# Three one-bank accumulators in place of one three-bank tile, and one block maximum a bank

## The chip, the cores and the metric

The kernel runs on one core of a Trainium2 chip. The core has a matrix engine (TensorE, PE in the profile, with its weight loads shown apart as PEld), a vector engine (VectorE, DVE), a scalar engine (ScalarE, ACT), GpSimd (POOL) and an engine that only issues DMAs here (SyncE, SP). The metric is the device time of one execution in microseconds; the kernel before takes 995.15 us (median of three runs, 993.82 to 997.5). Matrix products land in PSUM, which the kernel divides into eight banks of 512 float32 values a partition.

## What is computed

Block-sparse attention over 4 batches, 8 heads, 768 positions and head size 64, and then a feed-forward layer over all 3072 tokens:

```
scores = q @ k.T / 8, -1e9 where a 32x32 block isn't allowed
attn   = exp(scores - rowmax); attn /= attn.sum + 1e-9
x      = (attn @ v) as 3072 x 512
h      = x @ w_in                      # 512 x 2048
g      = h * clip(h + 3, 0, 6) / 6
out    = g @ w_out                     # 2048 x 512
```

All in float32. The kernel splits most float32 operands into a high part and a low remainder and adds three products. The subtraction of a row maximum is what the change touches on the attention side: before the exponentials of a head, the kernel needs for each query the largest allowed score, and gets it from maxima over the 24 blocks of 32 keys.

## The kernel before

**Units.** A unit is one head of one batch for one half (384) of its queries: 64 units, `u0` to `u63`. Its operations have short names. `m_0`, `m_1`, `m_2` are two matmuls each (128 queries by 2 times 384 keys); `r_0`, `r_1`, `r_2` are the VectorE reductions that take the 24 block maxima out of each (the tile `bm`); `fin_0` adds the mask row (`mq`), `fin_1` takes the maximum of the maxima (`mneg`); `mt` and `qm` carry it into an extra row of the query operand; `s`, `e` and `av` are scores, exponentials and the product with v; `suma` to `sumc` (tile `acc`) add up the denominator. `ql` (VectorE, tile `QA`) and `kl` (GpSimd, tile `kb`) compute low parts of the operands.

**Steps.** A step `m0` to `m63` is two column blocks of the feed-forward layer for one half of one batch: `h_..` (matmuls into `big`), `ga`, `gb`, `gh`, `gl` (the activation, on ScalarE, VectorE, ScalarE, GpSimd; tiles `g`, `ghi`, `glo`), and `o_tj` for three row tiles t and two blocks j: three matmuls that add into row tile t of the output. Eight steps accumulate into the same three row tiles; after the last of the eight, `oc_t` copies row tile t out of PSUM on VectorE (in the profile the copy `wraw<-out`, since it reuses that buffer), and `od_t` sends it to memory. The eight last steps of a group are `m7`, `m15`, and so on to `m63`.

**Weights.** 32 pieces of weight are taken apart early in the run (`w0` to `w31`, tiles `wraw` and `xhl`); this is VectorE and ScalarE work until about 212 us.

**Order.** The order is written out by hand in the long string SCORE. Each engine runs its instructions strictly in that order, each waiting on semaphores. The semaphores are set by the tile layer: it makes an instruction wait for earlier accesses to the same tile that it must not overtake.

**PSUM.** `big_tile()` gives one of two buffers of two banks (four banks), `avp` one bank, and `outp` three banks. In the kernel before, these three are one tile, `OUT` (`out` in the profile), made once at the top. It has three uses: the accumulators `OUT[:, t]` of the steps; the mask product of `mq` in its third bank; and for the early units `u1` to `u8` (where `self.early` holds) the two score halves of `m_t` in banks 0 and 1, so that these need no `big` buffer. In SCORE every early `m` comes after the `r` before it, since both use the same two banks.

All instructions are recorded through one helper, so nearly every row of the profile has its line (L357); rows are told apart by tile names and shapes.

Of the kernel before, what the change touches and what calls it, by code (L numbers as in the profile page):

```python
# [13 lines left out]
F32 = mybir.dt.float32  # L14
F32R = mybir.dt.float32r
I32 = mybir.dt.int32
AF = mybir.ActivationFunctionType
ALU = mybir.AluOpType
AX = mybir.AxisListType

P = 128
B, H, S, D = 4, 8, 768, 64
BLK = 32
NB = S // BLK
HALF = S // 2
NC = S // P
DM = H * D
# [4 lines left out]
NT = HALF // P  # L32
# [8 lines left out]
SCORE = """  # L41
# [286 lines left out]
def fused_kernel(ctx: ExitStack, tc, qT, kT, vP, sampled, w_in, w_out, krows, table, ident_d, out):  # L328
    nc = tc.nc
    const = ctx.enter_context(tc.tile_pool(name="const", bufs=1))  # L330
    sb = ctx.enter_context(tc.tile_pool(name="sb", bufs=2))
# [3 lines left out]
    outp = ctx.enter_context(tc.tile_pool(name="outp", bufs=1, space=bass.MemoryType.PSUM))  # L335

    def big_tile():
        return big.tile([P, 2, 512], F32, name="big")
# [20 lines left out]
    pe, dve, act, pool, dma = (Ordered(e) for e in (nc.tensor, nc.vector, nc.scalar, nc.gpsimd, nc.sync))  # L359
# [7 lines left out]
    eps_b = const.tile([P, 1], F32, name="eps_b")  # L367
    ones = const.tile([P, 32], F32, name="ones")
    MN = [const.tile([P, 2, NT], F32R, name=f"mneg{i}") for i in range(2)]
    OUT = outp.tile([P, NT, DM], F32, name="out")  # L370
    VO = [const.tile([P, 2 * NC * D], F32, name=f"vo{side}") for side in range(2)]

    def set_constants():
# [36 lines left out]
    class Masks(Work):  # L410
# [8 lines left out]
        def needs(self, op):  # L419
            return [(self, self.NEEDS.get(op, ""))]  # L420

        def heat(self):

            self.hot = sb.tile([P, 2, HALF], F32R, name="ghi")
            nc.gpsimd.memset(self.hot.bitcast(F32), 1.0)

        def warm(self, *number):
            for _ in range(number[-1]):
                pe.matmul(OUT[:, 2, :HALF], lhsT=self.hot[:, 0, :P], rhs=self.hot[:, 1], start=True, stop=True)

        def samp(self):
            self.sampled = const.tile([NB, 6], I32, name="samp")
            dma.dma_start(out=self.sampled, in_=sampled)
# [37 lines left out]
                dve.tensor_scalar(out=self.mval[:, 64:88], in0=msk, scalar1=1.0, scalar2=-NEG, op0=ALU.subtract, op1=ALU.mult)  # L471

        def mq(self):
            self.mqp = OUT[:, 2]
            for t in range(NC):
                pe.matmul(self.mqp[:, t * NB:(t + 1) * NB], lhsT=self.ind_f[:NB, t // NT * HALF + t % NT:(t // NT + 1) * HALF:NT], rhs=self.mval[:, 64:88].bitcast(F32), start=True, stop=True)

# [59 lines left out]
    class Unit(Work):  # L537
# [89 lines left out]

        def m(self, t):
            if self.early:
                ps = OUT[:, 0:2]  # L630
            else:
                ps = big_tile()
            self.mps = [*(self.mps if t else []), ps[:, :, :HALF]]
            for j in range(2):
                pe.matmul(ps[:, j, :HALF], lhsT=self.QA[:, t:HALF:NT], rhs=self.KA[:, j * HALF:(j + 1) * HALF], start=True, stop=True)

        def r(self, t):
            if t == 0:
                self.bm = sb.tile([P, NT, NB], F32, name="bm")
            bm = self.bm[:, t].rearrange("p (j n) -> p j n", j=2)  # L640
            dve.tensor_reduce(out=bm, in_=self.mps[t].rearrange("p j (n e) -> p j n e", e=BLK), axis=AX.X, op=ALU.max)

        def fin(self, i):
            if i == 0:
# [125 lines left out]
    moe_out = {}  # L770

    class Step(Work):
# [74 lines left out]

        def o(self, t, j):
            if self.fp == 0 and t == 0 and j == 0:
                moe_out[self.b, self.hf] = [OUT[:, t_] for t_ in range(NT)]  # L850
            o = moe_out[self.b, self.hf][t]
            f = 2 * self.fp + j
            for i, (lhs, rhs) in enumerate(((self.ghi, wout_hi[:, f]), (self.ghi, self.wo[j]), (self.glo, wout_hi[:, f]))):
                pe.matmul(o, lhsT=lhs[:, j, t * P:(t + 1) * P], rhs=rhs, start=f + i == 0, stop=f + i == NF + 1)
# [13 lines left out]
    masks = Masks()  # L868
# [22 lines left out]
            for op in ops:  # L891
                work.do(op)

    if "warm" in SCORE:
        masks.do("heat")
    set_constants()
    play(SCORE)

# [37 lines left out]
```

## Time and profile before

| | |
|---|---|
| median of three runs | 995.15 us |
| profiled execution, its own time | 994.87 us |
| its span, first to last instruction | 993.1 us |
| TensorE busy | 950.6 us (96%), clock 0.997 |
| VectorE busy | 642.3 us (65%), 900 instructions |
| ScalarE, GpSimd busy | 471.1 us, 249.9 us |
| chain that ended last | PE 80%, DVE 12%, ACT 3% |
| reductions from the early banks, `bm<-out` | 24, 954 ns each, 21.7 to 91.0 us |
| copies out of the accumulators, `wraw<-out` | 24, 686 ns each, 231.1 to 989.5 us |

A timeline row gives start, length, engine, operation, tiles and count, and in brackets the idle time of that engine just before it and whose end ended it. A row of the view of waits gives who waited for whom, the sum in us, how many times, and the longest. A busy TensorE is no proof of full use: matmuls overlap, so their pitch (from one start to the next) says more than their length.

### The profile page before, as it was taken

What the parts mean: (1) busy time and instruction counts of PE and PEld (TensorE: products, weight loads), DVE (VectorE), ACT (ScalarE), POOL (GpSimd) and SP (SyncE); (2) the same over time, 40 slices, a digit from 0 to 9 for tenths busy, and PEclk for the clock granted to TensorE, in tenths of its full rate; (3) what the DMA queues carried; (4) which work ended last, traced back from release to release, by engine and by line L of the source; (5) the groups of instructions that cost most, each with busy time, mean ns of one, the idle gap of its engine ahead of it and who ended that gap; (6) DMA issues with size and microseconds to landing.
All of it is one profiled execution on the core that took longest, in us unless ns stands there. A gap on an engine that the chain in (4) does not pass through costs nothing.

```text
span 993.1 us, 13262 instructions
## 1 busy us (share of the span) xinstructions
PE 950.6 (96%) x4756; PEld 767.9 (77%) x4756; DVE 642.3 (65%) x900; ACT 471.1 (47%) x712; POOL 249.9 (25%) x148
## 2 busy tenths in 40 slices
PE   6898999999999999999999999999999999999997
PEld 4566777778687878878878878887888787778886
DVE  5788898976768654777666674665666675752111
ACT  5787766463445344444553454444354543432121
POOL 3221222322223123232332233122222212302221
PEclk9899999999999999999999999999999999999999
DMA  6676977664444454535454455454543544515442
GB/s 199 193 244 210 273 267 236 202 220 147 144 139 139 123 165 132 155 111 165 142 153 132 131 152 163 124 154 134 170 147 108 149 131 138 145 48 146 142 118 72
DMA packets 103701, 155.48 MB, mean 157 GB/s; under 512 B 32819, under 2 KB 51891, under 8 KB 103636
## 3 DMA queue, kind: packets, MB, share of 16 engines
q1 hardware_dynamic: 103636, 154.64, 51.2%
q8 instruction: 37, 0.61, 0.3%
q14 instruction: 28, 0.23, 0.1%
HBM read 139.63 MB, written 14.78 MB: 155 GB/s over the span
## 4 chain that ended last, share of the span: by engine, by line
PE 80%; DVE 12%; ACT 3%; issue 3%; DMA 1%; POOL 0%; DVEq 0%; ACTq 0%
PE big L357 44%; PE out L357 25%; PE av L357 12%; DVE xhl L357 3%; DVE bm L357 3%; DVE acc L357 2%; DVE QA L357 2%; ACT pr L357 1%; ACT xhl L357 1%; DMA win_lo<-xhl 1%; DMA wout_lo<-xhl 1%; DVE wraw L357 0%; ACT qb L357 0%; DVE uu L357 0%; DMA qraw<-qT 0%
## 5 line engine op out<-in xcount | busy, mean ns | idle before, releaser
L357 PE MATMUL big<-xhl,win_hi 128*128 128x384 f32 x1024 | 265.0, 340 | 0.6 <-DVE bm L357 0.6
L357 POOL TENSOR_TENSOR glo<-g,ghi 128x768 fp32r<-128x768 f32 x64 | 120.2, 1878 | 430.3 <-ACT ghi L357 425.1
L357 ACT ACTIVATE pr<-big 128x768 f32<-128x768 f32 x192 | 153.0, 809 | 102.9 <-PE big L357 102.1
L357 POOL TENSOR_TENSOR kb<-kraw,KA 64x768 fp32r<-64x768 f32 x64 | 124.4, 1943 | 298.8 <-ACT KA L357 252.8
L357 PEld LDWEIGHTS big<-xhl,win_hi 128*128 128x128 f32 x1024 | 184.5, 188 | 14.3 <-issue 7.3
L357 DVE TENSOR_REDUCE bm<-big 128x24 f32<-128x768 f32 x168 | 158.0, 953 | 54.8 <-PE big L357 53.0
L357 PE MATMUL big<-xhl,wlo_in 128*128 128x384 f32 x512 | 172.3, 337 | 0.0
L357 PE MATMUL av<-pr,vo 128*64 128x384 f32 (+1 forms) x768 | 163.6, 494 | 0.1
L357 PE MATMUL out<-wout_hi,ghi 128*128 128x512 f32 x384 | 152.7, 398 | 5.8 <-DVE wraw L357 5.8
L357 PE MATMUL out<-wout_hi,glo 128*128 128x512 f32 x384 | 151.2, 394 | 0.6 <-POOL glo L357 0.6
L357 PE MATMUL out<-wlo_out,ghi 128*128 128x512 f32 x384 | 150.8, 393 | 0.0
L357 PE MATMUL big<-QA,KA 128*128 128x384 f32 x384 | 138.5, 361 | 3.1 <-ACT pr L357 1.3
L357 PE MATMUL big<-qb,kb 97*128 97x384 f32 x384 | 132.7, 345 | 3.9 <-ACT qb L357 3.2
L357 DVE SCALAR_TENSOR_TENSOR g<-g,big 128x768 f32<-128x768 f32 x64 | 60.8, 950 | 109.7 <-ACT g L357 109.3
L357 ACT ACTIVATE g<-big,half_b 128x768 f32<-128x768 f32 x64 | 57.7, 902 | 142.5 <-PE big L357 126.9
L357 PEld LDWEIGHTS av<-pr,vo 128*64 128x64 f32 (+1 forms) x768 | 67.6, 147 | 65.6 <-issue 50.5
L357 PE MATMUL big<-KA,QA 128*128 128x384 f32 x336 | 92.7, 367 | 13.9 <-ACT KA L357 5.1
L357 PEld LDWEIGHTS big<-KA,QA 128*128 128x128 f32 x336 | 74.8, 255 | 35.9 <-issue 8.8
L357 DVE TENSOR_TENSOR acc<-pr 128x768 f32<-128x768 f32 x52 | 54.3, 1045 | 68.1 <-ACT pr L357 67.8
L357 PEld LDWEIGHTS big<-xhl,wlo_in 128*128 128x128 f32 x512 | 96.2, 188 | 0.0
L357 PEld LDWEIGHTS big<-QA,KA 128*128 128x128 f32 x384 | 73.9, 192 | 23.8 <-ACT pr L357 7.7
L357 ACT CAST ghi<-g 128x768 fp32r<-128x768 f32 x64 | 53.3, 833 | 73.7 <-DVE g L357 48.5
(63 smaller groups left out, 977.2 us busy)
## 6 DMA issues: line engine op xcount, KB each, us to landing
wlo_out<-wout_lo SPq DMA_DIRECT2D x126, 256.0 KB, 2.8
wlo_in<-win_lo SPq DMA_DIRECT2D x126, 256.0 KB, 2.9
kraw<-kT SPq DMA_DIRECT2D x64, 384.0 KB, 3.5
qraw<-qT SPq DMA_DIRECT2D x64, 192.0 KB, 3.2
vo<-vP SPq DMA_DIRECT2D x64, 192.0 KB, 3.0
wraw<-w_in SPq DMA_DIRECT2D x16, 512.0 KB, 4.3
wraw<-w_out SPq DMA_DIRECT2D x16, 512.0 KB, 4.8
rec<-rec SPq DMA_DIRECT2D x64, 96.0 KB, 2.9
```

The costliest lines, as they stand in the source:

```text
L357: return lambda *a, **k: tc.keep_in_program_order(op(*a, **k))
```

## The change

`OUT` is gone. `outp` now hands out tiles of one bank each, by the names `out0`, `out1` and `out2`, with one buffer a name. The accumulators of a group of eight steps are three such tiles, made anew at the group's first `o_00`. The mask product takes `out0`. An early unit n takes two of the three names, beginning at `(n - 1) // 2 + 1` modulo 3 (units 1 and 2: out1 and out2; 3 and 4: out2 and out0; 5 and 6: out0 and out1; 7 and 8: out1 and out2), and each `m_t` asks for them anew. Its `r_t` becomes two reductions of 384 elements, one a bank, each written to its half of `bm`. The unused `warm` and `heat` helpers go, since they named `OUT`.

```diff
-    OUT = outp.tile([P, NT, DM], F32, name="out")
...
         def mq(self):
-            self.mqp = OUT[:, 2]
+            self.mqp = outp.tile([P, DM], F32, name="out0")
...
         def m(self, t):
             if self.early:
-                ps = OUT[:, 0:2]
+                bank = (self.n - 1) // 2
+                ps = [outp.tile([P, DM], F32, name=f"out{(bank + 1 + j) % NT}")[:, :HALF] for j in range(2)]
             else:
                 ps = big_tile()
-            self.mps = [*(self.mps if t else []), ps[:, :, :HALF]]
+            self.mps = [*(self.mps if t else []), ps if self.early else ps[:, :, :HALF]]
             for j in range(2):
-                pe.matmul(ps[:, j, :HALF], lhsT=self.QA[:, t:HALF:NT], rhs=self.KA[:, j * HALF:(j + 1) * HALF], start=True, stop=True)
+                out_j = ps[j] if self.early else ps[:, j, :HALF]
+                pe.matmul(out_j, lhsT=self.QA[:, t:HALF:NT], rhs=self.KA[:, j * HALF:(j + 1) * HALF], start=True, stop=True)
 
         def r(self, t):
...
-            dve.tensor_reduce(out=bm, in_=self.mps[t].rearrange("p j (n e) -> p j n e", e=BLK), axis=AX.X, op=ALU.max)
+            if self.early:
+                for j in range(2):
+                    dve.tensor_reduce(out=bm[:, j], in_=self.mps[t][j].rearrange("p (n e) -> p n e", e=BLK), axis=AX.X, op=ALU.max)
+            else:
+                dve.tensor_reduce(out=bm, in_=self.mps[t].rearrange("p j (n e) -> p j n e", e=BLK), axis=AX.X, op=ALU.max)
...
         def o(self, t, j):
             if self.fp == 0 and t == 0 and j == 0:
-                moe_out[self.b, self.hf] = [OUT[:, t_] for t_ in range(NT)]
+                moe_out[self.b, self.hf] = [outp.tile([P, DM], F32, name=f"out{t_}") for t_ in range(NT)]
```

No instruction changes its place among the others on any engine; only the reductions are doubled, and waits are other ones. Three places show it. In these rows `[waits X]` names the engines or DMA queues on whose semaphores an instruction waits, and numbers after `out` tell the new one-bank tiles apart.

The first place is TensorE in the early units: `m_2` of `u1`, then `m_0` of `u2`, the little transposes of `mt`, the first scores of `u1`, and `m_1` of `u2`. Before:

```order
L357 MATMUL out<-KA,QA 128x384 [waits DVE_49]
L357 MATMUL out<-KA,QA 128x384
L357 MATMUL out<-KA,QA 128x384 [waits DVE_49,Activation_49]
L357 MATMUL out<-KA,QA 128x384
L357 MATMUL big<-ident,mneg_118 2x128 [waits DVE_49,PE_49]
L357 MATMUL big<-ident,mneg_118 2x128 x2
```

and in the changed kernel:

```order
L357 MATMUL out_305<-KA,QA 128x384 [waits DVE_49]
L357 MATMUL out_306<-KA,QA 128x384 [waits DVE_49]
L357 MATMUL out_322<-KA,QA 128x384 [waits DVE_49,Activation_49]
L357 MATMUL out_323<-KA,QA 128x384 [waits DVE_49]
L357 MATMUL big<-ident,mneg_118 2x128 [waits DVE_49]
L357 MATMUL big<-ident,mneg_118 2x128 x2
```

Before, the first matmul of a pair waits for the whole reduction before it and the second for nothing more. Now each waits for the one reduction that read its own bank.

The second place is VectorE just before (`r_1` of `u1`, then the low part of a weight piece and `ql` of `u2`, as a difference):

```order
-L357 TENSOR_REDUCE bm<-out 128x24 [waits PE_49]
+L357 TENSOR_REDUCE bm<-out_286 128x12 [waits PE_49]
+L357 TENSOR_REDUCE bm<-out_287 128x12 [waits PE_49]
 L357 TENSOR_TENSOR wlo_out<-xhl,wout_hi 128x512 [waits Activation_49]
 L357 SCALAR_TENSOR_TENSOR QA<-qraw,QA 64x384 [waits DMAHW6_49]
```

The first reduction waits for the first matmul of the pair alone, the second for the second; the old one waited for both.

The third place is TensorE at the end of the program: the last step, `m63`, from the second matmul of `o_10` on (SCORE has there `o_10 oc_0 o_11 od_0 o_20 oc_1 o_21 od_1 oc_2 od_2`; an `o` is three matmuls). Before:

```order
L357 MATMUL out<-wlo_out,ghi 128x512
L357 MATMUL out<-wout_hi,glo 128x512
L357 MATMUL out<-wout_hi,ghi 128x512 [waits DVE_49]
L357 MATMUL out<-wlo_out,ghi 128x512
L357 MATMUL out<-wout_hi,glo 128x512
L357 MATMUL out<-wout_hi,ghi 128x512
L357 MATMUL out<-wlo_out,ghi 128x512
L357 MATMUL out<-wout_hi,glo 128x512
L357 MATMUL out<-wout_hi,ghi 128x512 [waits DVE_49]
L357 MATMUL out<-wlo_out,ghi 128x512
L357 MATMUL out<-wout_hi,glo 128x512
```

and in the changed kernel:

```order
L357 MATMUL out_8552<-wlo_out,ghi 128x512
L357 MATMUL out_8552<-wout_hi,glo 128x512
L357 MATMUL out_8552<-wout_hi,ghi 128x512
L357 MATMUL out_8552<-wlo_out,ghi 128x512
L357 MATMUL out_8552<-wout_hi,glo 128x512
L357 MATMUL out_8553<-wout_hi,ghi 128x512
L357 MATMUL out_8553<-wlo_out,ghi 128x512
L357 MATMUL out_8553<-wout_hi,glo 128x512
L357 MATMUL out_8553<-wout_hi,ghi 128x512
L357 MATMUL out_8553<-wlo_out,ghi 128x512
L357 MATMUL out_8553<-wout_hi,glo 128x512
```

Before, `o_11` (bank 1) waits for the copy `oc_0` (which reads bank 0), and `o_21` (bank 2) for `oc_1` (bank 1): the tile layer orders accesses to one tile, whatever bank of it they touch. The copies themselves wait likewise: by the semaphore counts, `oc_0` before waits for the last matmul of `o_10` and `oc_1` for that of `o_20`, each the last one issued into the tile; in the changed kernel `oc_0` waits for the last matmul of `o_01` and `oc_1` for that of `o_11`, the last into its own bank. Both waits of TensorE on a copy are gone. The same holds at the end of each group of eight: in all, eleven matmuls of an `o` lose a wait on a copy, and none gains one.

More of the change, by code (lines that the diff above doesn't have):

```diff
@@ L420, in needs @@
             return [(self, self.NEEDS.get(op, ""))]
[L422 to L429, printed above, removed]
         def samp(self):
@@ L892, in play @@
                 work.do(op)
-    if "warm" in SCORE:
-        masks.do("heat")
     set_constants()
```

## The prediction

> **What bounds the kernel now.** I read the table of busy time by stretches first, to see where TensorE is full.
>
> ```profile
> 20.00:93.00 73.00, 63.19 (x251) 45.93 (x250) 59.12 (x96) 55.92 (x92) 16.59 (x9) 0.95 0.68 217
> 93.00:180.00 87.00, 79.62 (x367) 62.37 (x366) 78.15 (x122) 57.06 (x92) 20.54 (x10) 1.00 0.80 253
> 180.00:585.00 405.00, 401.03 (x2079) 323.93 (x2078) 276.47 (x374) 191.97 (x289) 108.05 (x56) 1.00 0.49 149
> 930.00:983.00 53.00, 53.00 (x264) 47.48 (x263) 6.16 (x7) 11.27 (x13) 12.93 (x7) 1.00 0.38 109
> ```
>
> The columns are the stretch, its length, and then busy time of PE, PEld, DVE, ACT and POOL. From 180 us on TensorE is busy nearly all the time (401.03 of 405.00 us, 53.00 of 53.00), so a microsecond in which it stands still there is a microsecond of the program. Before that, several engines wait on each other: from 93 to 180 us VectorE is busy 78.15 of 87.00, and from 20 to 93 us nothing is full. The early units lie in that first stretch. Second came the view of waits, for everything that touches the three banks in question.
>
> ```profile
> DVE wraw L357 <- PE out L357: 23.4, 12, 7.8
> DVE bm L357 <- PE out L357: 10.5, 10, 3.2
> PEld out L357 <- DVE wraw L357: 8.1, 6, 2.0
> PE out L357 <- DVE wraw L357: 5.8, 6, 1.7
> PE out L357 <- DVE bm L357: 2.7, 3, 1.1
> ```
>
> Two of these rows belong to the early units: VectorE waits 10 times for early scores (10.5 us), TensorE 3 times for an early maximum (2.7 us). The two rows `<- DVE wraw` belong to the other end of the kernel: 6 times a matmul into an accumulator waits for a copy out of one. These 5.8 us of idle TensorE stand where it is the bound. The change names only the early maxima, but its one-bank tiles take these waits away too, and I expect most of the effect from there.
>
> **The late stalls.** The timeline has the six, each with the matmul ahead of it (second column: length, or that of so many together).
>
> ```profile
> 589.54 0.33 PE L357 MATMUL big<-xhl,wlo_in 128*128 128x384 f32 x1
> 590.84 0.50 PE L357 MATMUL out<-wout_hi,ghi 128*128 128x512 f32 x1 [0.97 <-DVE wraw L357]
> 593.24 0.69 DVE L357 COPY wraw<-out 128x512 f32<-128x512 f32 x1 [1.38 <-PE out L357]
> 819.62 1.83 POOL L357 TENSOR_TENSOR kb<-kraw,KA 64x768 fp32r<-64x768 f32 x1 [4.61 <-ACT KA L357]
> 819.67 2.20 DVE L357 TENSOR_TENSOR acc<-acc 128x384 f32<-128x384 f32 x1
> 820.98 0.52 PE L357 MATMUL big<-KA,QA 128*128 128x384 f32 x2
> 822.49 0.69 DVE L357 COPY wraw<-out 128x512 f32<-128x512 f32 x1
> 823.24 0.51 PE L357 MATMUL out<-wout_hi,ghi 128*128 128x512 f32 x1 [1.74 <-DVE wraw L357]
> 924.27 0.39 PE L357 MATMUL out<-wout_hi,glo 128*128 128x512 f32 x1
> 925.43 0.51 PE L357 MATMUL out<-wout_hi,ghi 128*128 128x512 f32 x1 [0.78 <-DVE wraw L357]
> 925.78 0.40 PE L357 MATMUL out<-wlo_out,ghi 128*128 128x512 f32 x1
> 926.01 0.39 PE L357 MATMUL out<-wout_hi,glo 128*128 128x512 f32 x1
> 926.71 0.39 PE L357 MATMUL out<-wout_hi,glo 128*128 128x512 f32 x1
> 927.88 0.50 PE L357 MATMUL out<-wout_hi,ghi 128*128 128x512 f32 x1 [0.78 <-DVE wraw L357]
> 984.86 0.39 PE L357 MATMUL out<-wout_hi,glo 128*128 128x512 f32 x1
> 986.03 0.50 PE L357 MATMUL out<-wout_hi,ghi 128*128 128x512 f32 x1 [0.78 <-DVE wraw L357]
> 987.29 0.40 PE L357 MATMUL out<-wout_hi,glo 128*128 128x512 f32 x1
> 988.47 0.50 PE L357 MATMUL out<-wout_hi,ghi 128*128 128x512 f32 x1 [0.78 <-DVE wraw L357]
> ```
>
> What one costs is the gap from start to start, less the pitch of an undisturbed stream, which is 0.23 us (925.78 to 926.01). The last four gaps are 1.16, 1.17, 1.17 and 1.18 us, so 0.93 to 0.95 too long; and the step after the stall is slow too (925.43 to 925.78 is 0.35, 0.12 over the pitch). That makes 1.05 us each, **4.2 us** for the four. At 590.84 the gap is 1.30 us against a pitch of some 0.17 to 0.23 and the same slow step: 1.2 us. At 823.24 the second of the two matmuls began 0.18 us into its row, near 821.16: a gap of 2.08, so **2.0 us**. This one is long because the copy came late: VectorE's sum at 819.67 took 2.20 us while GpSimd worked at 819.62 to 821.45, and the copy stood behind it. For the removal it doesn't matter why the copy is late, as the matmul no longer waits for it. Sum of the six: 4.2 + 1.2 + 2.0 = **7.4 us**.
>
> What is late next? At the four of the end nothing else ends in the stall: from 930 to 983 us TensorE is 53.00 of 53.00 busy and VectorE 6.16, so the activations follow the matmuls. After 590.84 and 823.24 VectorE has a backlog that does not move up with TensorE: behind the copy at 822.49 it still has a maximum and an activation to do, and what TensorE needs from these it now wants 1.2 or 2.0 us sooner. I take off 0.3 us in all for a wait that shows up there; the bounds are nothing and the whole 3.2 us of these two places. The end of the program:
>
> ```profile
> 986.00 4.51 SPq L357 DMA_DIRECT2D out_dram<-wraw  x3
> 989.46 0.69 DVE L357 COPY wraw<-out 128x512 f32<-128x512 f32 x1 [1.04 <-PE out L357]
> ```
>
> The three output transfers were issued over 4.51 us; they move together, to some 1.4 us apart (six matmuls at 0.23), and the last copy and its transfer still follow the last matmul. I take 0.1 us for transfers that are closer. Late part: −7.4 + 0.3 + 0.1 = **−7.0 us**, between −4.1 and −7.4.
>
> **The early part.** 24 reductions of 768 elements become 48 of 384. The price of one follows from two sizes of the same operation, and one pair of neighbours shows how soon the next instruction starts.
>
> ```profile
> L357 DVE TENSOR_REDUCE mneg<-bm 128x3 fp32r<-128x72 f32 x64 | 14.5, 226 | 2.0
> L357 DVE TENSOR_REDUCE bm<-out 128x24 f32<-128x768 f32 x24 | 22.9, 954 | 10.6 <-PE out L357 10.5
> 29.32 0.96 DVE L357 TENSOR_REDUCE bm<-out 128x24 f32<-128x768 f32 x1 [0.69 <-PE out L357]
> 30.20 0.42 DVE L357 TENSOR_SCALAR xhl<-xhl 128x512 int32<-128x512 int32 x1
> 56.44 0.80 PE L357 MATMUL out<-KA,QA 128*128 128x384 f32 x2
> 57.28 0.96 DVE L357 TENSOR_REDUCE bm<-out 128x24 f32<-128x768 f32 x1 [0.86 <-PE out L357]
> 58.29 0.68 PE L357 MATMUL out<-KA,QA 128*128 128x384 f32 x2 [0.88 <-DVE bm L357]
> ```
>
> (954 − 226) / (768 − 72) = 1.05 ns an element, so 226 − 75 = 151 ns are fixed, and a half costs 151 + 402 = 0.55 us. Two are 1.10 us busy against 0.954: 0.15 more, 3.6 us over 24. The next instruction starts 0.08 us before the end of the one ahead (29.32 + 0.96 = 30.28 against 30.20); where that holds between the halves too, a pair delays VectorE's queue by 0.07 us. [...]
>
> Against this stand two gains. Where VectorE waited for the pair of matmuls (10 of 24), the first half can start when the first matmul is done. From 56.44 the pair takes 0.80, of which one matmul is about 0.34 to 0.5, so the first half starts some 0.3 us sooner and the second ends at best 0.25 us sooner. Ten times 0.1 to 0.25 is 1 to 2.5 us. And where TensorE waited for a maximum (3 times, 2.7 us), it may start into the free bank half a reduction sooner: at 58.29 it would go on about 0.4 us earlier; three of these are about 1 us. In the other 14 pairs VectorE only pays, 14 × 0.07 = 1.0 us. All of it on the path gives −2.5 to +1.0; none of the gains and every pair at its full 0.15 gives +3.6; and with no engine full before 93 us part vanishes either way. I take **−0.5 us**. What is queued behind the added waits on TensorE is the next score or product with v, which runs when its own bank is free; the second matmul of a pair waits at most for the second half of a reduction, which would have held the whole pair before.
>
> **What could be redealt.** Two VectorE operations in this stage depend on who comes first.
>
> ```profile
> 55.60 0.56 DVE L357 SCALAR_TENSOR_TENSOR QA<-qraw,QA 64x384 fp32r<-64x384 f32 x1
> 56.01 1.82 POOL L357 TENSOR_TENSOR kb<-kraw,KA 64x768 fp32r<-64x768 f32 x1 [6.24 <-ACT KA L357]
> 72.94 1.81 POOL L357 TENSOR_TENSOR kb<-kraw,KA 64x768 fp32r<-64x768 f32 x1 [6.12 <-ACT KA L357]
> 73.09 2.07 DVE L357 SCALAR_TENSOR_TENSOR QA<-qraw,QA 64x384 fp32r<-64x384 f32 x1
> ```
>
> At 55.60 `QA` starts before GpSimd's subtraction and takes 0.56 us; at 73.09 it starts 0.15 us after GpSimd and takes 2.07, and ends just after it: 1.5 us lost. A shift of 0.2 us of either queue can win or lose such a race. [...]
>
> **The sum.** −7.0 − 0.5 = −7.5 us. The profiled execution took 994.87 us (span 993.1 and 1.8 around it), so its like comes to 987.4, and the span to 985.6. The median of the runs is 0.3 above that execution: **987.7 us**.
>
> **The rivals.** (A) *Only the end pays.* At 590 and 823 us VectorE's backlog becomes the next wait and holds TensorE for what it gained there, and the early stage keeps a cost. For it: TensorE's stall at 823 ends a chain of VectorE work that stays. Against it: VectorE is idle for 1.38 us ahead of the copy at 593.24, so its backlog there is short. 995.15 − 4.1 + 1 gives 992. (B) *Slower: races with GpSimd are lost in the early stage.* VectorE carries 0.07 to 0.15 us more for each pair, so its two-input operations start later and fall behind the start of GpSimd's subtractions, 9 of which lie in 20 to 93 us and 10 in 93 to 180. Each lost race costs 1.5 us (73.09) if it lies on the path. For it: from 93 to 180 us VectorE is nearly full. Against it: some races are lost already, and where VectorE waited for scores it now comes sooner. It takes five lost races with the full 3.6 us to undo the late gain (5 × 1.5 + 3.6 = 11.1 against 7.0 makes +4), so it decides from about three on: five give 999. (C) *The races are won.* With the one at 73.09 and another, and both early gains in full: 987.7 − 3 − 2 = 983. (D) *Just the early stage changes*, since waits also hide in a tile's release and the new tile's first matmul could wait for all three copies: then the time is 994.7. Against it: the instruction order shows none of these matmuls with a wait on VectorE.
>
> **How the numbers follow.** A measurement of this kernel tells some 0.5% (5 us) from no change: below 990.2 is faster, above 1000.1 slower. The forecast has a chance of 0.74, with an own range of 985 to 990; A 0.14, B 0.03, C 0.07, D 0.02. Faster: C and nearly all of the forecast, 0.79. Same: A, D, part of the forecast's edge and of B, 0.19. Slower: the far part of B, 0.02. The range takes in C's nearer half and most of A: 984.0 to 992.0.
>
> **What would show it.** (1) No row of `PE out <- DVE wraw` in the waits, and the last step's `out` matmuls at a pitch of 0.23 us from 984 us of the old time on: if that fails, D. (2) 48 reductions near 0.55 us, and fewer than 10.5 us of `DVE bm <- PE out`; if the time up to the first full stretch (180 us) moves by over 3 us, it was B or C. (3) From about 935 us on, everything some 6 us earlier than before. The forecast is wrong if a wait of TensorE on `bm`, `g` or `pr` of over 1 us comes up after 590 us, or if the first copy out of an accumulator, at 231.1 us before, comes more than 2 us later.

## The result, and the profile after

The changed kernel took 992.22 us (median of 12 runs, 989.39 to 994.18), the kernel before on the same chip 996.75 us (12 runs, 993.82 to 1001.6). The ratio is 0.995 with a 95% interval of 0.9936 to 0.9964: about 4.5 us less, at the bound of what was to be told from no change. The profiled execution took 989.39 us with a span of 987.6.

The view of waits of the changed kernel, in the rows that answer to those shown of before (who waits for whom, us in all, times, longest):

```profile
DVE wraw L357 <- PE out L357: 15.5, 7, 7.1
DVE bm L357 <- PE out L357: 9.0, 8, 3.0
PE out L357 <- DVE bm L357: 2.8, 4, 1.7
DVE wraw L357 <- DMA out_dram<-wraw: 1.6, 2, 0.8
```

The row in which an `out` matmul waits for a copy `wraw` is gone from TensorE. VectorE's waits for early scores fell only from 10.5 to 9.0 us, TensorE's for early maxima not at all. The last row is new: two copies wait until their buffer has been sent out.

The timeline of the changed kernel at the six late places, and at its end (start, length, then what ran):

```profile
590.85 0.33 PE L357 MATMUL big<-xhl,wlo_in 128*128 128x384 f32 x1
591.02 0.39 PE L357 MATMUL out<-wout_hi,ghi 128*128 128x512 f32 x1
...
820.75 0.52 PE L357 MATMUL big<-KA,QA 128*128 128x384 f32 x2
821.11 0.40 PE L357 MATMUL out<-wout_hi,ghi 128*128 128x512 f32 x1
819.44 2.08 DVE L357 TENSOR_TENSOR acc<-acc 128x384 f32<-128x384 f32 x1
822.14 0.69 DVE L357 COPY wraw<-out 128x512 f32<-128x512 f32 x1
822.75 0.95 DVE L357 TENSOR_REDUCE bm<-big 128x24 f32<-128x768 f32 x1
823.75 0.62 PE L357 MATMUL big<-xhl,win_hi 128*128 128x384 f32 x2 [0.73 <-DVE bm L357]
...
922.97 0.39 PE L357 MATMUL out<-wout_hi,glo 128*128 128x512 f32 x1
923.19 0.39 PE L357 MATMUL out<-wout_hi,ghi 128*128 128x512 f32 x1
...
924.34 0.39 PE L357 MATMUL out<-wout_hi,glo 128*128 128x512 f32 x1
924.57 0.39 PE L357 MATMUL out<-wout_hi,ghi 128*128 128x512 f32 x1
...
981.43 0.39 PE L357 MATMUL out<-wout_hi,glo 128*128 128x512 f32 x1
981.65 0.39 PE L357 MATMUL out<-wout_hi,ghi 128*128 128x512 f32 x1
...
982.80 0.39 PE L357 MATMUL out<-wout_hi,glo 128*128 128x512 f32 x1
983.03 0.39 PE L357 MATMUL out<-wout_hi,ghi 128*128 128x512 f32 x1
981.88 3.18 SPq L357 DMA_DIRECT2D out_dram<-wraw  x3
984.01 0.69 DVE L357 COPY wraw<-out 128x512 f32<-128x512 f32 x1 [0.78 <-DMA out_dram<-wraw]
```

Where the four gaps of 1.16 to 1.18 us stood at the end, matmuls now follow each other at 0.22 or 0.23 us. But 2.6 us after the removed stall of 823 us a new one stands: TensorE waits 0.73 us for a maximum, which VectorE does behind a copy (822.14, 822.75), and the copy behind a slow sum.

Set side by side instruction by instruction, TensorE of the changed kernel is up to 2.8 us ahead at 58 us, level at 145 us, 1.3 us behind at 206, level at 591, and then gains in steps to 5.45 us at the end. Most of the lead at 58 us is not the split's: the record of the granted clock has TensorE of the kernel before at half clock from 27.7 to 34.6 us, where the lead grew by 2.1 us, and TensorE of the changed kernel at full clock there and at half clock for 3.41 us each at 85.8 and 123.3 us, where the lead shrank again. The loss at 206 us is a wait on a small transfer, which both kernels issue at the same time (the kernel before, then the change; SPq is SyncE's DMA queue):

```profile
204.83 0.44 PE L357 MATMUL big<-qb,kb 97*128 97x384 f32 x1
...
200.63 0.48 SPq L357 DMA_DIRECT2D qb<-mneg  x1
```

```profile
206.17 0.45 PE L357 MATMUL big<-qb,kb 97*128 97x384 f32 x1 [1.16 <-DMA qb<-mneg]
...
200.65 0.48 SPq L357 DMA_DIRECT2D qb<-mneg  x1
```

So the late half shows the expected gain, and the early half nets nothing in this pair of executions. Whether that is the split's doing or chance, one pair cannot tell.

### The profile page after: what moved, and what is told of

Read it like the earlier page. It is cut to its first block, busy times and chain, and to the rows that moved or that the text cites. A ratio compares the mean times of both kernels' runs of the same rounds, so it can differ in the third digit from the quotient of the medians.

```text
span 987.6 us, 13284 instructions
## 1 busy us (share of the span) xinstructions
PE 950.8 (96%) x4756; PEld 768.8 (78%) x4756; DVE 643.5 (65%) x924; ACT 471.4 (48%) x712; POOL 249.5 (25%) x148
## 4 chain that ended last, share of the span: by engine, by line
PE 83%; DVE 9%; DMA 3%; ACT 3%; issue 2%; SPq 0%; DVEq 0%; ACTq 0%
PE big L357 45%; PE out L357 25%; PE av L357 13%; DVE bm L357 2%; DVE QA L357 2%; DVE acc L357 2%; DVE xhl L357 2%; ACT pr L357 1%; DMA wlo_out<-wout_lo 1%; DMA wraw<-w_out 1%; DMA qb<-mneg 1%; DMA win_lo<-xhl 1%; ACT qb L357 0%; ACT xhl L357 0%; DMA spread<-rec 0%
```

## The experiments

**The theory** after this comparison: the gain is the late waits of TensorE on copies, and the early split is worth about nothing. **Rival one:** the split costs, and the late gain covers it. **Rival two:** the split helps by itself. The first four kernels take the two parts apart. The instruction order of each differs from its base only in the waits concerned (and in the reductions, where these are split).

In what follows a stretch of TensorE is from the start of one of its instructions to the start of another, counted from zero in the order of the trace, which is the same in all of these kernels. The kernel before took 997.56, 996.07 and 995.89 us in the three sets of runs below.

### Separate accumulators alone

```diff
-    outp = ctx.enter_context(tc.tile_pool(name="outp", ...))
+    first = ExitStack(); outp = [first.enter_context(tc.tile_pool(name="outp", ...))]
...   # OUT, the early units and mq as before the change
-                moe_out[self.b, self.hf] = [OUT[:, t_] for t_ in range(NT)]
+                if self.n == 0:
+                    first.close()
+                    outp[0] = ctx.enter_context(tc.tile_pool(name="outp1", ...))
+                moe_out[self.b, self.hf] = [outp[0].tile([P, DM], F32, name=f"out{t_}") for t_ in range(NT)]
```

> The kernel before with only the accumulators of the steps in three separate banks; the early units keep the two-bank maximum of the kernel before. By the instruction order it differs from the kernel before only in waits that are gone. Theory (all of the gain is the late waits of TensorE on the copies, the early split is worth about 0): same as the change in one run of the same chip within 1.5 us, ratio to before 0.994 to 0.996, that is -4 to -6 us; in its trace the four stalls of the end (1.05 us each in the profile before) are gone and the first copy of an accumulator stands within 1.2 us of the 231.13 us of before. Rival one (the early split costs by itself, because two reductions take 1.02 us of VectorE where one took 0.95, and the late gain covers that): this kernel is 1.5 to 3 us faster than the change, ratio 0.992 to 0.993. Rival two (the split helps by itself, since a half is read while the other bank is written): this kernel gains only 2 to 3 us, ratio 0.997 to 0.998.

Measured: 991.68 us, ratio 0.9942 [0.9922, 0.9963].

### The early split alone

The other way round: the early units and `mq` as in the change, and from `m0` on one three-bank tile in a pool of its own.

```diff
-                moe_out[self.b, self.hf] = [outp.tile([P, DM], F32, name=f"out{t_}") for t_ in range(NT)]
+                if not late:
+                    first.close()
+                    late.append(ctx.enter_context(tc.tile_pool(name="outp1", ...)).tile([P, NT, DM], F32, name="out"))
+                moe_out[self.b, self.hf] = [late[0][:, t_] for t_ in range(NT)]
```

> The change with only its early part: 48 maxima of one bank each in the early units, and the accumulators of the steps in one three-bank tile as before. Theory (early split worth about 0): ratio to before 0.999 to 1.001, 0 +- 1 us; the six waits of TensorE on the copies are back, 1.05 us each at the four places of the end, 1.2 to 2 us at the two before. Rival one (the split costs, the late gain covers it): ratio 1.0015 to 1.003, +1.5 to +3 us, and the first copy of an accumulator (231.13 us before) comes over 1.2 us later. Rival two (the split gains by itself): 0.997 to 0.998, -2 to -3 us, first copy earlier by that much. If the 1.1 us that TensorE lost at 206 us in the profile of the change, on the transfer of the negated maxima, belongs to the split, it is seen here too at the same instruction; if it is a matter of that one execution, it need not be.

Measured: 999.4 us, ratio 1.001 [0.9991, 1.0028]. In its view of waits the six are back:

```profile
PE out L357 <- DVE wraw L357: 5.7, 6, 1.6
```

### The change once more

> The change itself once more, on the chip of the two halves, so that they are compared with it and not with other days. Expected by every theory: 0.994 to 0.996 of before. It tells apart what belongs to the change and what to one execution: the theory holds the wait of 1.16 us on the transfer of the negated maxima at 206 us, and the places of the two stretches of half clock (85.76 and 123.31 us in the first profile of the change), to be of that one execution, so that they stand elsewhere or are missing here; the reading that the change causes them has both again at the same instructions.

Measured: 992.34 us, ratio 0.9945 [0.9926, 0.9964]. The three results agree: the separate accumulators alone give what the change gives (0.9942 and 0.9945), and the split alone gives nothing that stands out of its interval (1.001). Rival two falls. Rival one's 1.5 us fits the intervals too, so that was still open. The time of the first copy, a sign named before, doesn't settle it: it came at 233.47 us with the separate accumulators alone, 2.3 us later than before and not within 1.2, and at 236.75 with the split alone, which would speak for rival one; but the six profiles of this document without the split have it anywhere from 228.5 to 238.2 us.

The wait on `qb<-mneg` near 206 us is a matter of the execution: 1.2 us in the first profile of the change, 0.8 in this one. Of all the profiles of this document, eight of fourteen have it, with 0.8 to 1.4 us: three of the six without the split and five of the eight with it. The spells of half clock stood at other places this time, at 31.7 and 437.9 us.

The late stretches, on the other hand, repeat to 0.2 us, also in the other profiles where nothing was edited in them (us):

| TensorE's instructions | at | one tile: before, split alone | separate: alone, change, again |
|---|---|---|---|
| 2745th to 2770th | 590 us | 6.35, 6.37 | 5.25, 5.05, 5.06 |
| 3930th to 3960th | 823 us | 7.43, 7.31 | 6.43, 6.42, 6.44 |
| 4450th to 4475th | 925 us | 7.47, 7.48 | 5.34, 5.34, 5.34 |
| 4740th to the span's end | 986 us | 9.58, 9.58 | 7.57, 7.56, 7.57 |

With about 1.2, 0.95, 2.13 and 2.0 us the late part is worth **6.3 us**. The whole way from the 2745th instruction to the span's end says the same, with more scatter: 404.6 and 404.3 us with one tile, 397.8 to 398.6 in the three others.

### One group back on one tile

```diff
+                if group == 7:
+                    whole = outp[0].tile([P, NT, DM], F32, name="out")
+                    moe_out[self.b, self.hf] = [whole[:, t_] for t_ in range(NT)]
+                else:
                     moe_out[self.b, self.hf] = [outp[0].tile([P, DM], F32, name=f"out{t_}") for t_ in range(NT)]
```

> The change with only the last group of steps (m56 to m63) put back on one three-bank tile. By the instruction order it differs from the change in two waits of TensorE on the copies that are back, at the two last blocks of the output matmuls (986.03 and 988.47 us in the profile before). Theory (each of those waits is paid in full, nothing behind it hides it): the two stalls are back with 1.0 to 1.1 us each, the end of the run comes 2.1 us later than the change on the same chip less at most 0.8 us, since the wait of the third copy for its output buffer (0.78 us in the change) vanishes behind the stall; as a ratio to before 0.996 to 0.998. Rival (the stalls at the end are hidden by the copies and output transfers, which set the end): same as the change within 0.5 us and the last transfer of the output ends no later.

Measured: 992.48 us, ratio 0.995 [0.9932, 0.9969], 0.14 us over the change's second set. The expected 0.996 to 0.998 was missed, though the interval reaches into it: the spread of whole runs hides 2 us. The trace decides. Its timeline at the end:

```profile
981.93 0.39 PE L357 MATMUL out<-wout_hi,glo 128*128 128x512 f32 x1
983.11 0.50 PE L357 MATMUL out<-wout_hi,ghi 128*128 128x512 f32 x1 [0.78 <-DVE wraw L357]
983.44 0.39 PE L357 MATMUL out<-wlo_out,ghi 128*128 128x512 f32 x1
...
984.37 0.40 PE L357 MATMUL out<-wout_hi,glo 128*128 128x512 f32 x1
985.55 0.50 PE L357 MATMUL out<-wout_hi,ghi 128*128 128x512 f32 x1 [0.78 <-DVE wraw L357]
...
986.54 0.69 DVE L357 COPY wraw<-out 128x512 f32<-128x512 f32 x1 [1.05 <-PE out L357]
```

Both stalls are back with gaps of 1.18 us, while in the other groups they stay away, and the last stretch takes 9.58 us again instead of 7.57. So each false wait is paid at the end of the program, and none is hidden by the output transfers.

### Doses of the early split

The next two kernels turn up what rival one holds against the split: VectorE's added time.

```diff
-                for j in range(2):
-                    dve.tensor_reduce(out=bm[:, j], in_=self.mps[t][j]...)
+                for j in range(4):
+                    dve.tensor_reduce(out=bm[:, j // 2, j % 2 * 6:j % 2 * 6 + 6], in_=self.mps[t][j // 2][:, j % 2 * 192:j % 2 * 192 + 192]...)
```

> The change with each early maximum cut once more: four reductions of 128x192 a pair of banks, 96 in all. From 954 ns for 768 elements and 551 for 384 a piece of 192 should take about 0.35 us, so that four take 1.4 us where two took 1.1 (both as sums of busy time): 3.5 to 7 us more of VectorE in 24 pairs. Theory (what VectorE does in the early stage is absorbed in waits on transfers, so the early split is worth about 0): ratio to before 0.994 to 0.997, that is at most 1.5 us over the change in the same call, and the late places unchanged (1.05 us less at each of the four ends than before). Rival (VectorE's early time is paid, and the split of the change cost 1 to 2 us of the late gain): +3.5 to +7 us against the change, ratio 0.998 to 1.0015, with the first copy of an accumulator later by as much.

The second has eight pieces of 96 elements in the same way.

> The change with each early maximum in eight reductions of 128x96 a pair, 192 in all, the next dose after four. Groups of the profiles so far: 24 reductions take 22.9 us in all, 48 take 24.5, 96 take 27.6, so about 0.15 us for the start of each; 192 should take 1.05 ns for an element and 0.148 us each, 0.249 us a piece and 48 us in all, 23 us more than the change. Theory (after the four-way split: VectorE's early time is paid at least in part, the wait for transfers at 140 to 206 us doesn't take it up): +12 to +23 us against the change, ratio 1.006 to 1.018. Rival (the loss of the four-way split was a collision or a transfer of its own, VectorE's time is absorbed): under +6 us, ratio below 1.001.

Measured: four, 994.73 us, ratio 0.9987 [0.9975, 1.0]; eight, 1000.09 us, ratio 1.0059 [1.0037, 1.0081]. The groups of reductions (count, then busy time in all, ns of one, idle time before them) of the change, of four and of eight:

```profile
L357 DVE TENSOR_REDUCE bm<-out 128x12 f32<-128x384 f32 x48 | 24.5, 551 | 9.3 <-PE out L357 9.0
```

```profile
L357 DVE TENSOR_REDUCE bm<-out 128x6 f32<-128x192 f32 x96 | 27.6, 350 | 8.2 <-PE out L357 7.9
```

```profile
L357 DVE TENSOR_REDUCE bm<-out 128x3 f32<-128x96 f32 x192 | 33.6, 246 | 7.6 <-PE out L357 7.4
```

The busy time counts overlapping instructions once. From 22.9 us for 24 whole reductions each added piece costs 1.6 / 24, 4.7 / 72 and 10.7 / 168 us, which is 0.064 to 0.067 us each time, though the length of one falls by less than its share (two of 551 ns are 148 ns longer than one of 954). My expectation for eight multiplied counts by lengths and overlooked that neighbours overlap; its 23 us more than the change are in truth 9.1.

Against the separate accumulators alone (0.9942), the ratios make +0.3 us for two pieces, +4.5 for four and +11.7 for eight, each 2 to 3 us uncertain. VectorE's added busy time is 1.6, 4.7 and 10.7 us. Against the change in its second set, four is 4.2 us slower, where the rival had 3.5 to 7 and the theory at most 1.5; eight is 11.4 slower, a little under the 12 to 23 that rested on the wrong busy time. So more pieces cost time: the theory's second half falls, and rival one was right about the kind of thing. For the two pieces of the change the +0.3 us cannot be told from nothing.

Whether the price is VectorE's queue time alone these two kernels don't show, since they also lose more collisions with GpSimd, the subject of the next section. From 20 to 100 us the kernel before has two operations of VectorE that start behind GpSimd's `kb` and take at least 0.9 us longer than elsewhere (`bm` at 38.39 us with 1.73 us against 0.22, `QA` at 73.09 with 2.07 against 0.56); the change has three (`bm` at 36.23 with 1.74, `xhl` at 62.34 with 2.16 against 0.54, `QA` at 71.81 with 2.18), the kernel with four pieces four, and the one with eight pieces six. The added queue time and the added collisions grow together.

### A collision of VectorE with GpSimd

One early row differs in all four profiles with two pieces and the order of the change from the four without the split, the added operation and the swaps below. VectorE's difference `xhl` of unit 1 and GpSimd's `kb`, in the kernel before and in the change:

```profile
64.59 0.55 DVE L357 TENSOR_TENSOR xhl<-uu,xhl 128x384 fp32r<-128x384 f32 x1
64.59 2.23 POOL L357 TENSOR_TENSOR kb<-kraw,KA 64x768 fp32r<-64x768 f32 x1 [6.76 <-ACT KA L357]
```

```profile
62.34 2.16 DVE L357 TENSOR_TENSOR xhl<-uu,xhl 128x384 fp32r<-128x384 f32 x1
62.28 1.81 POOL L357 TENSOR_TENSOR kb<-kraw,KA 64x768 fp32r<-64x768 f32 x1 [6.68 <-ACT KA L357]
64.78 0.34 PE L357 MATMUL big<-ident,mneg 128*2 128x128 f32 x3 [1.31 <-DVE spread L357]
```

Before, VectorE started in the same hundredth of a microsecond and went through in 0.55 us. In the change it starts 0.06 us after GpSimd, takes 2.16, and TensorE waits 1.31 us for what is queued behind it (`mneg`). The reduction ahead of it is the one that takes 0.06 us longer in two pieces. GpSimd's `kb` takes 2.23 us where VectorE went through and 1.81 where VectorE started behind it, 0.42 us less. With four and eight pieces VectorE is later still, so that the same `kb` catches the operation ahead of `xhl` instead. In the kernel of four:

```profile
66.57 1.80 POOL L357 TENSOR_TENSOR kb<-kraw,KA 64x768 fp32r<-64x768 f32 x1 [6.36 <-ACT KA L357]
66.71 1.76 DVE L357 TENSOR_TENSOR bm<-bm,mq 128x72 f32<-128x72 f32 x1
68.39 0.55 DVE L357 TENSOR_TENSOR xhl<-uu,xhl 128x384 fp32r<-128x384 f32 x1
```

Two kernels test what this is worth: in one an added operation makes VectorE lose the collision with no split, in the other the split stays and `mneg` goes ahead of the collision.

```diff
 # lost: separate accumulators, early units unsplit
+                if self.n == 1: dve.tensor_reduce(out=sb.tile([P, NT], F32, name="idle", bufs=1), in_=units[5].bm, axis=AX.X, op=ALU.max)
                 dve.tensor_tensor(out=xs[self.pair][:, 1], ...)
```

> The separate accumulators alone, early units as before, with one added operation of 0.2 us on VectorE (a maximum of the sums that nothing reads) ahead of the difference xhl of unit 1, so that this difference starts behind GpSimd's kb and not at the same time as it. In the three profiles without the split and without swaps both start within 0.01 us of each other and the difference takes 0.55 us; in the split ones it starts 0.06 us behind and takes 2.16. Theory (what the split costs early is this collision, 1.2 us of TensorE between its 60th and 200th instruction): xhl takes 1.9 to 2.2 us here too, and that stretch goes from 38.2-38.4 to 39.5-39.9 us without any split; time 0.5 to 2 us above the separate accumulators alone. Rival (the split's early cost is its own VectorE time): xhl may be late, but the stretch stays under 38.8.

```diff
 # race_fix: the change with two swaps in SCORE
-u1 ux_2; u5 fin_1; u6 kl;
+u5 fin_1; u1 ux_2; u6 kl;
...
-u7 ql; w10 high; u6 fin_1; u7 kl;
+u6 fin_1; u7 ql; w10 high; u7 kl;
```

> The change with two neighbours swapped on VectorE: the negated maximum of a unit (0.2 us, mneg) is done ahead of an operation on two buffers that lies beside a difference on GpSimd (64.8 and 74.3 us in the profile of the change with the last group put back; 2.16 and 2.19 us there, 0.55 us where nothing lies beside it). TensorE waits for mneg. Expected by every theory: mneg some 1.6 to 1.9 us earlier at both places, and TensorE's transposes behind it too. Theory (early time is given back behind the transfers of the weights and of the negated maxima between 140 and 206 us): ratio to before 0.9935 to 0.9955, within 1 us of the change. Rival (early time goes through to the end, so that the collision at 64.8 us, which all four profiles with the split show and no profile without it, is a price of the split): 1.5 to 3 us faster than the change, ratio 0.991 to 0.993.

Measured: lost, 993.86 us, ratio 0.997 [0.9951, 0.9988]; with the swaps, 990.39 us, ratio 0.9941 [0.9919, 0.9963]. The first one's timeline on VectorE and GpSimd:

```profile
67.19 0.23 DVE L357 TENSOR_REDUCE idle<-bm 128x3 f32<-128x72 f32 x1
67.33 1.95 DVE L357 TENSOR_TENSOR xhl<-uu,xhl 128x384 fp32r<-128x384 f32 x1
67.07 1.80 POOL L357 TENSOR_TENSOR kb<-kraw,KA 64x768 fp32r<-64x768 f32 x1 [6.76 <-ACT KA L357]
69.57 0.34 PE L357 MATMUL big<-ident,mneg 128*2 128x128 f32 x3 [1.30 <-DVE spread L357]
```

The stretch that I had named, from the 60th to the 200th instruction, takes 39.91 us, but a spell of half clock begins in its last part, so I read a shorter one: from the 60th instruction to the transposes of `mneg` (the 185th). Executions with 3.4 to 4.1 us of half clock at its beginning:

| | 60th to 185th, us |
|---|---|
| no split, collision won: before, separate alone, late edits | 34.53, 34.64, 34.42 |
| no split, collision lost by the added operation | 36.31 |
| split alone, collision lost | 36.17 |
| split, `mneg` ahead of it: swaps, all edits | 34.12, 34.41 |

The collision is worth 1.5 to 2.1 us there, with the split or without; the split costs nothing there when `mneg` goes ahead. Two executions at full clock over the whole stretch agree: 34.57 us in the first profile of the change, 32.98 in the second of the late edits below, which has no split and wins the collision. What is left of it later I can't say so exactly. From the 185th to the 290th instruction the second profile of the change takes 29.0 us and the kernel before and the separate accumulators alone 29.7 to 29.8, all at full clock, so 0.7 us is caught up there. The lost kernel, which is unsplit, and the split alone each have two spells of half clock in that stretch and take 31.6 and 31.5 us, so this gain seems to follow the collision and not the split. From 121 to 206 us ScalarE waits for transfers of weight pieces, 6.4 us in the kernel before and 6.1 in the change, and executions of one kernel differ by 1 to 2 us. The ratios of these kernels lie too close for their intervals: 0.997 of the lost one against 0.9942 without the loss would be 2.8 us, more than the 0.5 to 2 expected, but the intervals overlap; and 0.9941 against 0.9945 is within the theory's range, while its interval reaches into the rival's too.

### The late leftovers, and all edits together

The two new waits of the late part, on the separate accumulators without the split:

```diff
-m47 oc_1; u60 m_0; m47 o_21 od_1; u60 r_0;
+u60 m_0; m47 o_21; u60 r_0; m47 oc_1 od_1;
...
-                self.ot[t] = sb.tile([P, DM, 2], F32, name="wraw")...
+                self.ot[t] = (sb.tile([P, 2, HALF], F32, name="g", bufs=1)... if (self.n, t) == (63, 2) else sb.tile([P, DM, 2], F32, name="wraw")...)
```

> The separate accumulators alone (early units as before), with two late edits: near 822 us one maximum goes ahead of a copy of an accumulator on VectorE, since TensorE waited 0.73 us for that maximum in the change; and the third copy of the last step goes to another buffer, since it waited 0.78 us for the transfer out of the first copy. Theory (what is left of the late false waits is these two): the stretch of TensorE from its 3930th to its 3960th instruction, 7.43 us before and 6.43 with separate accumulators, falls to 5.6 to 5.9; from the 4740th to the end, 9.58 and 7.57, to 6.7 to 7.0; 1.4 us in all against the separate accumulators alone, ratio to before 0.992 to 0.994. Rival (the wait at 823.75 has another cause behind it, the output transfer's time sets the end): no difference, 0.994 to 0.995.

Measured: 990.03 us, ratio 0.9944 [0.9924, 0.9964], in the rival's range and just over the theory's, with an interval that reaches into both. The stretch at 823 us fell from 6.43 to 5.42 us. The one at the end fell from 7.57 only to 7.47, not to 6.7 to 7.0. The last copy in this kernel:

```profile
981.43 0.69 DVE L357 COPY g<-out 128x512 f32<-128x512 f32 x1 [0.75 <-PE out L357]
```

Its idle time is 0.75 us again, now ended by TensorE. The 0.78 us of the change had been ended by the transfer, but the last matmul ends only 0.1 us sooner than that, so nothing more was to be had.

> The separate accumulators with the two late edits once more, on the chip of the three others, as their base: 0.993 to 0.995 by every theory. Its trace tells how far the stretch of TensorE from its 520th to its 780th instruction (55.0 to 56.7 us so far, ended by the wait for the transfer of the negated maxima at 204 to 211 us) goes by chance: the theory that it is chance expects another value here than the 55.15 of the first profile of this kernel, or the wait for that transfer with another length.

Measured: 989.68 us, ratio 0.9946 [0.9926, 0.9966]. The stretch at 823 us takes 5.89 us here. In the first execution VectorE's sum (`acc`) started 0.08 us before GpSimd's `kb` and took 0.56 us; in the last kernel below, where the stretch also takes 5.89 us, it starts 0.12 us after `kb` and takes 2.13. From the 520th to the 780th instruction this kernel takes 56.14 us against 55.15, so that part is chance, as expected.

> The last kernel with the two swaps of VectorE's order in the early part added. Theory: as that kernel within 1 us, since early time is given back; with one thing apart from it: without the split the operation at 64.6 us already won its collision, so at that place there is nothing to gain, and at 73.1 us about 1.5 us. Rival (early time goes through): 1 to 1.5 us faster than that kernel, ratio to before 0.990 to 0.992.

Measured: 992.17 us, ratio 0.9956 [0.9939, 0.9974]: no gain in the time from the swaps without the split. At the first place there was none to be had, since there the collision is won without them (34.56 us to the 185th instruction). At the second, at 73 us, TensorE takes 11.89 us from the 185th to the 230th instruction against 12.70 in the kernel before and 12.69 in the first profile of the late edits, so 0.8 us came of the expected 1.5; the intervals of the whole times are too wide to show it.

> The change with all small edits tried: both swaps of the negated maximum in the early stage, the maximum ahead of the copy near 822 us and the other buffer for the last copy. Theory: the stretches of TensorE as measured alone, 60th to 200th instruction 38.0 to 38.4 us (39.5 with the split and the collision lost), 3930th to 3960th 5.4, 4740th to the end 7.5; ratio to before 0.992 to 0.9945, some 1 to 2 us under the change. Rival (early order is worth nothing at the end): 0.9935 to 0.995, same as the separate accumulators with the late edits in this call.

Measured: 989.14 us, ratio 0.9934 [0.9908, 0.9959], the lowest ratio of all, with 34.41 us to the 185th instruction, 38.24 to the 200th and 7.46 at the end, as expected; the 5.89 us at 823 are 0.5 over it, with the sum of 2.13 us. It beats the kernel before by 0.4 to 0.9%. Over the change (0.9945 and 0.995) the intervals overlap, so that it is better than that is likely from the stretches, and not shown by the times.

## Why the prediction was right, and where it was off

The prediction was right in its main point: the change names the early maxima, and its effect comes from the late waits, which the one-bank tiles take away. The kernels with one part each show it (0.9942 and 1.001). The size was too large. The forecast of 987.7 us was 4.5 us too low, the median lies just over its range's upper end of 992.0, and the time under 990.2 us that had a chance of 0.79 did not come. Of the 4.5 us, 1.6 is the base: the kernel before ran at 996.75 us in the twelve runs beside the change, against the 995.15 of the runs I had. The other 3.0 us is the gain, forecast at 7.5 and measured at 4.5: 0.7 of it in the late part and 2.3 in the early part. Step by step:

- **The four stalls of the end, 4.2 us:** right. The stretches give 2.13 and 2.0, and putting one group back brings 2.0 us back.
- **590 us, 1.2 us:** right, 1.1 to 1.3. VectorE's backlog there made no new wait.
- **823 us, 2.0 us, less 0.3 for a wait behind VectorE's backlog:** the mechanism was foreseen and its size was too small. TensorE gained 0.9 to 1.0 us and not 1.7, since 0.73 us of waiting for a maximum came up in its place. VectorE's sum of 2.08 us beside GpSimd stays, the copy follows it and the maximum follows the copy; taking the maximum ahead of the copy got 0.5 us back where the sum took 2.13 us, and 1.0 where it took 0.56. This is rival A's mechanism, at one place of two.
- **Closer output transfers, 0.1 us of loss:** right, 2.1 us for the two stalls against 2.0 at the end. The copy's new wait for its buffer added at most 0.1.
- **The early part, −0.5 us:** the weakest step. The price of a half (0.55 us) was right, and so was 0.07 us of delay in the queue for a pair: 0.067 measured. But the gains of 2 to 3.5 us from waits did not come: VectorE's wait for early scores fell by 1.5 us in the first profile of the change and by nothing in that of the split alone, TensorE's for early maxima by nothing. And a collision that rival B describes was lost, as far as the rows tell because of those 0.06 us, at 1.5 to 2.1 us. It was one, not five, and 0.7 us of it was caught up soon after. The doses cost 4.5 and 11.7 us in all, where VectorE's added time is 4.7 and 10.7, which doesn't bear out my argument that part of it vanishes since no engine is full before 93 us; how much of the cost is the queue and how much further collisions stays open.
- **Sum:** −6.3 for the late part; the remaining +1.8 of the measured −4.5 us is the early part together with what executions scatter by. The runs of the single parts put the split at +0.3 and +1.0 us, each with an uncertainty of 2 us or more, so the cause of the whole +1.8 is not shown.

Rival D is refuted by the waits. C is refuted by the collisions: one more was lost, and the one that it would have won, `QA` at 73.09 us, stayed lost in the change (2.18 us). Rival A's 992 us meets the measured number, but partly by luck: on the base of the twelve runs A would come to 993.6 and the forecast to 989.3, and the measured 992.22 lies between them; of A's two late places only one came, and that in part.

By the lengths, a second piece costs 0.148 us (two of 551 ns against one of 954); as queue time the doses show less than half of it, 0.064 to 0.067 us, since neighbours overlap: two halves in a row take 1.02 us and not 1.10.

Of my signs, the waits on copies are gone and VectorE's wait for scores is under 10.5 us, but from 935 us on TensorE was 3.4 us earlier than before and not some 6. For a wrong forecast, the time of the first copy was a bad sign: it came 0.64 us late in the first profile of the change (231.77 us) and 5.75 in the second, while the 930th instruction of TensorE, close by, stands anywhere from 232.6 to 242.3 us in profiles of kernels that differ little.

## What to carry to other kernels

In this tile layer one tile over several banks makes accesses to different banks wait for each other; look for an engine at its bound that waits for a copy out of a neighbour's bank, and price each such wait by the gap in its stream less the pitch. In a stretch in which one engine never stands still such a gap is paid in full at the end, so it can be summed in advance (4.2 us for the four at the end, 4.1 measured), unless another engine's backlog becomes the next wait, as at 823 us. Where several engines wait on each other, 0.06 us can turn over a collision and cost 1.5 us or more, and only a run tells. When the change is smaller than the spread of whole executions, compare the same stretch of one engine between two fixed instructions, over several profiles.

## What the runs showed of the hardware that I had not expected

TensorE's granted clock falls to half (0.5 in its record) for short spells in the middle of the run, at other places in each execution. The table of stretches, of the change and then of the separate accumulators alone (the third column from the right is the granted clock):

```profile
430.00:440.00 10.00, 8.66 (x44) 8.01 (x45) 6.98 (x11) 1.74 (x2) 0.00 (x0) 1.00 0.59 184
```

```profile
430.00:440.00 10.00, 8.26 (x35) 7.45 (x34) 5.88 (x8) 0.00 (x0) 0.90 (x1) 0.83 0.41 131
```

By the record of the granted clock, each such spell lasts 3.41 or 6.83 us, and the times between them are multiples of 3.41 (399.36 us is 117 of them). The spell near 434 us appears in 7 of the 14 profiles, after the same stop of TensorE (1.6 us, for `bm`), and costs 1.5 us: from the 1900th to the 1960th instruction 14.2 us without it, 15.8 with. On the grid of 3.41 us that the changes of the clock lie on, the stop began between 0.1 us before and 0.61 us after a grid point in all seven with the spell, and 1.25 to 2.94 us after one in all seven without. So the phase of a short stop goes together with whether it costs 1.5 us more, and an edit that shifts the program by a microsecond could turn that over; I didn't shift it on purpose, so this is seen, not shown to be the cause.

The profile of the change had no spell near 28 us, where most others have 3.41 to 6.83 us, and two at 86 and 123 us.
